# Where a linear-attention block places its last feature-map rows and num/den tiles among the units of the output projection

## The chip, the core and the metric

The kernel runs on one core of a Trainium2 chip. A core has five engines that run side by side, each with its own in-order stream of instructions: TensorE (PE) multiplies matrices, VectorE (DVE), ScalarE (ACT) and GpSimd (POOL) work on elements, SyncE (SP) here only issues DMAs. ACT issues some DMAs too. The metric is the device time of one execution in microseconds; lower is better.

## The reference

`x` is 2048 tokens by 1024 features. It is normalised once, and two blocks read the result:

```python
qkv = (xn @ wqkv)                 # 32 heads of 32
phi = lambda t: where(t > 0, t + 1, exp(t)) + 1e-6
pq, pk = phi(q), phi(k)
kv  = einsum("bhsd,bhse->bhde", pk, v)      # over all tokens
z   = einsum("bhsd->bhd", pk)
num = einsum("bhqd,bhde->bhqe", pq, kv)
den = einsum("bhqd,bhd->bhq", pq, z)[..., None] + 1e-6
s   = (num / den) @ wo                       # heads put side by side again
g   = silu((silu(xn @ w_gate) * (xn @ w_up)) @ w_down)
out = x + s * g
```

Since `kv` and `z` are sums over all tokens, no `num` can be made before the keys and values of the last token are there.

## The kernel before

**Stages.** First the normalisation, K and V for 16 token tiles of 128, and six of the eight Q groups (lines 255 to 596). Then, in lines 598 to 720, the stage that the change is in: the last two Q groups, num/den, and the output projection of the attention. Then the gate, up and down projections (lines 728 to 1064), which take most of the time.

**Q groups.** A `QGroup` (line 205) makes 256 of the 1024 columns of q for 1024 tokens by a seven-product scheme, as phi(q) transposed, in a tile `pqT`. `part_a`, `part_b` and `part_c` issue 8, 12 and 8 matmuls of 128x512; ACT makes exp and relu of the results (lines 186, 187), DVE the sums between them (lines 231, 236, 246). `part_d(i)` closes one of the two rows of 128 columns: `emit_phi` (line 189), two DVE instructions on 128x1024. The two groups of this stage are `qa` and `qb`, the third and fourth column groups of the second half of the tokens.

**num/den tiles.** `emit_ND(b, t)` (line 621) makes one token tile: eight matmuls of 128x132 (line 632) into three PSUM tiles `nd_ps`, all three buffers of the pool `psA`; then on DVE three additions (line 636), a reciprocal (line 639) and three multiplications out of PSUM (line 642) into `o_sb`. The next tile's matmuls need those three buffers back. There are 16 tiles, called tile 0 to 15 below. Tiles 0 to 7 read `pqT` of the first half of the tokens, tiles 8 to 15 that of the second half, `qa` and `qb` included.

**The way to the projection.** `emit_OT` (line 651) takes every finished `o_sb`: ACT issues a write to DRAM (`o_dram`, line 655), SP then issues a transposing DMA back into SBUF (line 656; into `oT` for tiles 0 to 7, into the space of `wq_sb` for 8 to 15). After tile 15 it also puts the first three pairs of gate and up weights into SP's queue (`load_w`, line 658).

**Units.** `emit_S(b, t, cc)` (line 661) is one unit of the output projection: eight matmuls of 128x512 (line 669) for one token tile and one half of the columns, then an ACT cast to `s_sb`; the second unit of a tile also issues the write of `s_sb` on ACT's queue. Units 0 to 31 run in order; unit u reads the transposed tile u//2. Their PSUM comes from `psB`, five buffers, shared with the Q groups.

**Order.** In lines 689 to 720 the order of the instructions on PE, DVE, ACT, POOL and SP is that of the text (`manual_schedule`). `units` and `nds` are the queues of what is still to be issued. Before the loop three tiles are taken; in the loop a tile goes ahead of a unit unless the number of units left is 2 modulo 4, where up to two of the three rows left over stand instead:

```python
rows = deque(((qa, 1), (qb, 0), (qb, 1)))
while units:
    if len(units) % 4 != 2:
        nd_tile()
    else:
        for _ in range(min(2, len(rows))):
            grp, i = rows.popleft()
            grp.part_d(i)
```

So tiles 3 to 15 stand ahead of units 0, 1, 3, 4, 5, 7, 8, 9, 11, 12, 13, 15 and 16; the row (qa, 0) ahead of `qb.part_b`, (qa, 1) and (qb, 0) ahead of unit 2, (qb, 1) ahead of unit 6. `sum_w(0, 0)` and `sum_w(0, 1)` (line 166, DVE sums of the first gate and up weights) stand ahead of unit 28 in both kernels.

Of the kernel before, what the change touches and what calls it, by code (L numbers as in the profile page):

```python
# [21 lines left out]
def kernel(  # L22
# [119 lines left out]
    def x_operands(p):  # L142
        xs, xn_ = XS[p], xnT[p]
        return {"M4": lambda k: xs[:, 0, k, :], "M3": lambda k: xs[:, 1, k, :], "M1": lambda k: xs[:, 2, k, :],
                "N7": lambda k: xs[:, 3, k, :], "N6": lambda k: xs[:, 4, k, :],
                "M5": lambda k: xn_[:, HD + k, TB:2 * TB], "M2": lambda k: xn_[:, k, 0:TB]}
# [19 lines left out]
    def sum_w(m, gu):  # L166
        wsum[(m, gu)] = ws_all[:, m % 2, gu]
        for op in wsum_ops(wraw[(m, gu)], wsum[(m, gu)]):
            op()

    def w_operands(m, gu):
        return block_operands(wraw[(m, gu)], wsum[(m, gu)])

    def load_w(m, after=None, sync=False):
        cols = slice(m * FW, (m + 1) * FW)
        wg_sb = wgu.tile([P, DC, FW], BF16, name="wg_sb", tag="wg_sb")
        d1 = nc.sync.dma_start(out=wg_sb[:], in_=wg_v[:, :, cols])
        wu_sb = wgu.tile([P, DC, FW], BF16, name="wu_sb", tag="wu_sb")
        d2 = nc.sync.dma_start(out=wu_sb[:], in_=wu_v[:, :, cols])
        gate([d1, d2], after, sync=sync)  # L180
        wraw[(m, 0)] = wg_sb
        wraw[(m, 1)] = wu_sb
# [72 lines left out]
    with ExitStack() as p1:  # L255
# [242 lines left out]
        with tc.manual_schedule(engines=FRONT_ORDER):  # L498
# [69 lines left out]
            for i in range(TPB, NT):  # L568
                grp = QGroup(*early.popleft()) if i >= Q0 and early else None
# [28 lines left out]
    with ExitStack() as p2:  # L598
# [9 lines left out]
        def oT_of(b):  # L608
            return (oT_ab[:] if b < 2 else oT_cd)[:, b % 2]

        def emit_KVZ():
            for j in range(NJ):
                g0 = j * GPT
                ng = min(GPT, G - g0)
                nc.vector.tensor_tensor(out=KVZ[:, g0:g0 + ng, 0:P], in0=kvz_ps[j][:, 0:ng, 0:P],
                                        in1=mask[:, None, :].to_broadcast([P, ng, P]), op=ALU.mult)
                nc.vector.tensor_tensor(out=KVZ[:, g0:g0 + ng, P:P + HPG],
                                        in0=kvz_ps[j][:, 0:ng, P:P + 1].to_broadcast([P, ng, HPG]),
                                        in1=sel[:, None, :].to_broadcast([P, ng, HPG]), op=ALU.mult)
# [31 lines left out]
        def emit_OT():  # L651
            while o_ready:
                b, t, o_sb = o_ready.popleft()
                r0 = b * TB + t * P
                nc.scalar.dma_start(out=o_dram[r0:r0 + P, :], in_=o_sb[:])
                nc.sync.dma_start_transpose(out=oT_of(b)[:, :, t * P:(t + 1) * P], in_=o_dram[r0:r0 + P, :])
                if (b, t) == (NB - 1, TPB - 1):
                    for m in range(PREF):
                        load_w(m)
# [19 lines left out]
        units = deque((b, t, cc) for b in range(NB) for t in range(TPB) for cc in range(NCC))  # L679
        nds = deque((b, t) for b in range(NB) for t in range(TPB))  # L680

        def s_unit():
            emit_S(*units.popleft())

        def nd_tile():
            if nds:
                emit_ND(*nds.popleft())

        with tc.manual_schedule(engines=FRONT_ORDER | {ET.SP}):

            qa, qb = (QGroup(NPASS - 1, m) for m in (NM_Q - 2, NM_Q - 1))
            for c in range(NCC):
                nc.sync.dma_start(out=wo_sb[:, :, c * CW:(c + 1) * CW], in_=wo_v[:, :, c * CW:(c + 1) * CW])
            emit_KVZ()
            qa.part_a()
            qa.part_b()
            nd_tile()
            qb.part_a()
            emit_OT()
            qa.part_c()  # L700
            nd_tile()
            qa.part_d(0)
            qb.part_b()
            emit_OT()
            nd_tile()
            qb.part_c()
            emit_OT()
            rows = deque(((qa, 1), (qb, 0), (qb, 1)))
            while units:
                if len(units) % 4 != 2:  # L710
                    nd_tile()
                else:
                    for _ in range(min(2, len(rows))):
                        grp, i = rows.popleft()
                        grp.part_d(i)
                if len(units) == 2 * NCC:
                    sum_w(0, 0)
                    sum_w(0, 1)
                s_unit()
                emit_OT()  # L720
    p12.close()
    ps12.close()

# [207 lines left out]
    with tc.manual_schedule(engines=PE_ORDER):  # L931
        prev = None
        for m, p in order:
# [15 lines left out]
            for gu in range(2):  # L949
                sink = gs if gu == 0 else UpSink(gs, m, p)  # L950
                grp = Group(w_operands(m, gu), x_operands(p), HD, sink)
# [92 lines left out]
    with tc.manual_schedule(engines=PE_ORDER):  # L1044
# [9 lines left out]
        for j in range(NPAIR):  # L1054
            grp = nxt
# [39 lines left out]
```

## Time and profile before

| what | value |
|---|---|
| median of three runs | 758.9 us (758.7 to 759.54) |
| the profiled execution's own time | 758.81 us |
| its span, first to last instruction | 757.0 us |
| PE busy / DVE / ACT / POOL | 746.9 / 482.1 / 276.5 / 50.9 us |
| PE, 179.49 to 191.00 us (end of `qb.part_c` to unit 4) | 10.34 of 11.51 us busy |
| PE, 191.00 to 217.00 us (the other tiles) | 25.84 of 26.00 us busy |
| PE, 217.00 to 244.25 us (units alone) | 27.14 of 27.25 us busy |
| granted TensorE clock | 1.00 in these three windows |
| first matmul of the gate projection | 244.25 us |

A profile is of one execution. The span leaves 1.81 us of that execution's time outside. The profile counts a matmul as busy for longer than its share of the array (378 ns where the next one starts 216 ns later), so two matmuls overlap, and what PE loses is better read from the starts than from the busy share.

### The profile page before, as it was taken

Reading aid. Unit: us, or ns where it says so; the run is one execution under the profiler, and the core shown is the slowest. Engines: PE = TensorE matmul, PEld = TensorE weight load, DVE = VectorE, ACT = ScalarE, POOL = GpSimd, SP = SyncE. Lnnn points to the kernel's source line nnn. Section 1 sums busy time; section 2 is a strip of 40 time slices with the busy share of each in tenths; the row PEclk is TensorE's granted clock in tenths of the full one; section 3 lists DMA queues with packets and bytes.
Section 4 is the critical chain, followed back from the end, with each engine's and each line's share of the span. In section 5 each row is a group of like instructions: output and inputs, shape, how many; then the busy total and the mean of one; then the engine's idle time right before and its main releaser. Section 6 shows DMA issues by size and latency. Waiting matters only on the chain.

```text
span 757.0 us, 9915 instructions
## 1 busy us (share of the span) xinstructions
PE 746.9 (99%) x3724; PEld 351.7 (46%) x3764; DVE 482.1 (64%) x897; ACT 276.5 (37%) x482; POOL 50.9 (7%) x112
## 2 busy tenths in 40 slices
PE   8999999999999999999999999999999999999997
PEld 4544444444544444444444444444444444444454
DVE  6686666349843577776787777776755744445453
ACT  4444556555223434343433334343443111111111
POOL 3311000000000000000000000000000112222220
PEclk9999999999999999999999999999999999999999
DMA  9606100016899334573354634543869854554200
GB/s 318 223 16 184 40 1 0 1 45 186 237 234 287 115 102 146 165 217 110 93 174 147 202 107 131 170 150 112 298 225 352 299 181 181 181 178 171 96 29 29
DMA packets 127663, 115.98 MB, mean 153 GB/s; under 512 B 29440, under 2 KB 108416, under 8 KB 126336
## 3 DMA queue, kind: packets, MB, share of 16 engines
q1 hardware_dynamic: 122720, 106.58, 44.8%
q10 hardware_dynamic: 4896, 8.78, 3.5%
q8 instruction: 29, 0.48, 0.3%
q14 instruction: 18, 0.15, 0.1%
HBM read 70.52 MB, written 38.54 MB: 144 GB/s over the span
## 4 chain that ended last, share of the span: by engine, by line
PE 95%; DVE 3%; issue 1%; DMA 0%; ACT 0%; DVEq 0%; ACTq 0%
PE X L131 29%; PE Y L131 28%; PE kv_ps L428 14%; PE Z L131 10%; PE s_ps L669 6%; PE qY L131 3%; PE qX L131 3%; PE kvz L457 1%; PE nd_ps L632 1%; DVE o_sb L642 1%; PE qZ L131 1%; DVE stats L322 0%; PE tr_ps L397 0%; DMA xp<-in_A_x_dram 0%; DVE pqT L191 0%
## 5 line engine op out<-in xcount | busy, mean ns | idle before, releaser
L131 PEld LDWEIGHTS <-ws_all 128*128 128x128 bf16 x1420 | 137.8, 98 | 162.6 <-issue 0.2
L758 DVE TENSOR_TENSOR q<-n,Y 128x512 f32<-128x512 f32 x63 | 43.4, 688 | 116.8 <-PE Y L131 105.8
L428 PE MATMUL kv_ps<-wkv_sb,xnT 128*128 128x512 bf16 x496 | 114.2, 379 | 1.2 <-DVE xnT L411 0.5
L131 PEld LDWEIGHTS <-xs 128*128 128x128 bf16 x616 | 58.0, 98 | 63.1
L1028 POOL TENSOR_TENSOR o_out<-y,xres 128x512 bf16<-128x512 f32 x29 | 33.5, 1157 | 652.4 <-DVE y L1027 652.4
L428 PEld LDWEIGHTS <-xnT 128*128 128x128 f16 x512 | 49.3, 98 | 57.6 <-DVE xnT L411 0.7
L131 PE MATMUL Y<-xs,ws_all 128*128 128x512 f16 (+3 forms) x308 | 70.3, 360 | 0.0
L131 PE MATMUL X<-xnT,ws_all 128*128 128x512 f16 (+1 forms) x278 | 70.1, 379 | 0.2
L131 PE MATMUL Z<-xs,ws_all 128*128 128x512 f16 x224 | 57.5, 379 | 0.0
L131 PE MATMUL Y<-xnT,ws_all 128*128 128x512 f16 x224 | 57.5, 379 | 0.0
L131 PE MATMUL X<-xs,ws_all 128*128 128x512 f16 x224 | 57.5, 379 | 0.0
L882 ACT ACTIVATE g<-cg 128x512 bf16<-128x512 f32 x56 | 35.4, 633 | 53.9 <-DVE cg L773 53.9
L764 DVE TENSOR_TENSOR u<-Z,q 128x512 f32<-128x512 f32 x63 | 43.3, 688 | 16.0 <-PE Z L131 15.9
L882 ACT ACTIVATE g<-X 128x512 bf16<-128x512 f32 x28 | 16.7, 598 | 99.3 <-PE X L131 99.2
L754 ACT COPY n<-X 128x512 f32<-128x512 f32 x63 | 37.0, 587 | 28.2 <-PE X L131 27.8
L907 DVE TENSOR_TENSOR ho<-g,up 128x1024 bf16<-128x1024 bf16 x56 | 38.3, 686 | 0.5
L131 PEld LDWEIGHTS <-wg_sb 128*128 128x128 bf16 x224 | 21.9, 98 | 26.6 <-issue 0.3
L673 ACT CAST s_sb<-s_ps 128x512 bf16<-128x512 f32 x32 | 18.4, 587 | 43.4 <-PE s_ps L669 29.5
L131 PEld LDWEIGHTS <-wu_sb 128*128 128x128 bf16 x224 | 21.9, 98 | 26.4
L1027 DVE TENSOR_TENSOR y<-y,s_in 128x512 f32<-128x512 f32 x31 | 21.3, 686 | 20.2 <-ACT y L1021 15.9
L1021 ACT ACTIVATE y<-X 128x512 f32<-128x512 f32 x8 | 4.8, 598 | 69.7 <-PE X L131 61.2
L186 ACT ACTIVATE e_t<-kv_ps 128x512 bf16<-128x512 f32 x32 | 19.2, 600 | 29.6 <-PE kv_ps L428 27.2
(140 smaller groups left out, 1046.1 us busy)
## 6 DMA issues: line engine op xcount, KB each, us to landing
h_dram<-ho SPq DMA_DIRECT2D x56, 256.0 KB, 2.5
wg_sb<-in_B_w_gate_dram SPq DMA_DIRECT2D x14, 512.0 KB, 4.0
wu_sb<-in_B_w_up_dram SPq DMA_DIRECT2D x14, 512.0 KB, 4.0
wdr<-in_B_w_down_dram SPq DMA_DIRECT2D x14, 512.0 KB, 4.0
ws_all<-h_dram SPq DMA_DIRECT2D x4, 1792.0 KB, 8.3
wds_dram<-wdsA SPq DMA_DIRECT2D x14, 384.0 KB, 2.6
hp_a<-h_dram SPq DMA_DIRECT2D x3, 1792.0 KB, 9.0
o_dram<-o_sb ACTq DMA_DIRECT2D x16, 256.0 KB, 3.1
```

The lines of the kernel that those rows point to most:

```text
L131: marks["mm"] = nc.tensor.matmul(acc[:, 0:c1 - c0], lhsT=lhs(k), rhs=rhs(k)[:, c0:c1], start=(first and k == 0), stop=(k == n - 1), skip_g ...
L186: nc.scalar.activation(out=e, in_=t, func=ACT.Exp)
L428: mm = nc.tensor.matmul(kv_ps[:], lhsT=xn_tok_ap(i)[:, dc, :], rhs=wkv_sb[:, dc, c * CW:(c + 1) * CW], start=(dc == 0), stop=(dc == DC - 1))
L669: mm = nc.tensor.matmul(s_ps[:], lhsT=oT[:, c, ttok], rhs=wo_sb[:, c, cc * CW:(cc + 1) * CW], start=(c == 0), stop=(c == G - 1))
L673: nc.scalar.copy(out=s_sb[:, cc * CW:(cc + 1) * CW], in_=s_ps[:])
L754: nc.scalar.copy(out=n[:], in_=self.X[:])
L758: nc.vector.tensor_tensor(out=self.q[:], in0=n[:], in1=self.Y[:], op=ALU.add)
L764: nc.vector.tensor_tensor(out=self.u[:], in0=Z[:], in1=self.q[:], op=ALU.add)
L882: nc.scalar.activation(out=self.g[:, i, j * TB:(j + 1) * TB], in_=src, func=ACT.Silu)
L907: nc.vector.tensor_tensor(out=self.ho[:, i], in0=self.g[:, i], in1=self.up[:, i], op=ALU.mult)
L1027: nc.vector.tensor_tensor(out=t[:], in0=t[:], in1=self.s_in[:, i, cs], op=ALU.mult)
L1028: (nc.vector if last and (i, j) != (0, 0) else nc.gpsimd).tensor_tensor(out=self.o_out[:, i, cs], in0=t[:], in1=self.xres[:, i, cs], op=AL ...
```

## The change

Three statements move; no instruction is added or dropped.

```diff
             qa.part_c()
             nd_tile()
-            qa.part_d(0)
             qb.part_b()
...
-            rows = deque(((qa, 1), (qb, 0), (qb, 1)))
+
+            rows = deque((grp, i) for grp in (qa, qb) for i in range(2))
+            nd_at = {1, 2, 4, 6, 8, 10, 11, 12, 14, 15, 16, 18, 19}
+            row_at = {3, 5, 7, 9}
+            assert len(nd_at) == len(nds) and len(row_at) == len(rows)
+            u = 0
             while units:
-                if len(units) % 4 != 2:
+                if u in nd_at:
                     nd_tile()
-                else:
-                    for _ in range(min(2, len(rows))):
-                        grp, i = rows.popleft()
-                        grp.part_d(i)
+                if u in row_at:
+                    grp, i = rows.popleft()
+                    grp.part_d(i)
                 if len(units) == 2 * NCC:
                     sum_w(0, 0)
                     sum_w(0, 1)
                 s_unit()
                 emit_OT()
+                u += 1
```

Tiles 3 to 15 now stand ahead of units 1, 2, 4, 6, 8, 10, 11, 12, 14, 15, 16, 18 and 19. Unit 0 follows `qb.part_c` with nothing between. The four rows stand one each ahead of units 3, 5, 7 and 9. The writes, the transposes and the weight loads that hang on the tiles move with them.

## The prediction

> **What bounds the kernel now.** I read the page first, then the chain of waits over this stage, the waits, PE's timeline, DVE's timeline, and the DMA issues one at a time.
>
> ```profile
> span 757.0 us, 9915 instructions
> PE 746.9 (99%) x3724; PEld 351.7 (46%) x3764; DVE 482.1 (64%) x897; ACT 276.5 (37%) x482; POOL 50.9 (7%) x112
> ```
>
> PE is the bound nearly everywhere; only what PE loses can be won. The waits from 179 to 217 us say where that is: PE waits for the multiplications that empty the num/den buffers.
>
> ```profile
> PEld L632 <- DVE o_sb L642: 3.5, 9, 0.9
> ...
> PE nd_ps L632 <- DVE o_sb L642: 0.7, 2, 0.4
> ```
>
> PE's timeline gives the places (start, length, what):
>
> ```profile
> 179.98 1.09 PE L632 MATMUL nd_ps<-KVZ,pqT 128*128 128x132 bf16 x8 [0.33 <-DVE o_sb L642]
> 180.91 1.89 PE L669 MATMUL s_ps<-wo_sb,oT 128*128 128x512 bf16 x7
> 183.18 1.08 PE L632 MATMUL nd_ps<-KVZ,pqT 128*128 128x132 bf16 x8 [0.39 <-DVE o_sb L642]
> 184.10 3.61 PE L669 MATMUL s_ps<-wo_sb,oT 128*128 128x512 bf16 x16
> 187.55 0.63 PE L632 MATMUL nd_ps<-KVZ,pqT 128*128 128x132 bf16 x8
> 188.02 1.89 PE L669 MATMUL s_ps<-wo_sb,oT 128*128 128x512 bf16 x8
> 189.82 1.08 PE L632 MATMUL nd_ps<-KVZ,pqT 128*128 128x132 bf16 x8
> ```
>
> Tile 5 (187.55) costs PE 0.47 us, start to start; tiles 3, 4 and 6 cost far more. DVE's timeline says why:
>
> ```profile
> 176.90 0.42 DVE L190 TENSOR_SCALAR e_t<-e_t 128x1024 bf16<-128x1024 bf16 x1
> 177.42 0.69 DVE L191 TENSOR_TENSOR pqT<-e_t,pqT 128x1024 bf16<-128x1024 bf16 x1
> 178.03 0.68 DVE L236 TENSOR_TENSOR qu<-qu,qZ 128x512 f32<-128x512 f32 x1
> 178.63 0.31 DVE L636 TENSOR_SCALAR rden<-nd_ps 128x12 f32<-128x12 f32 x3
> 178.98 0.35 DVE L639 RECIPROCAL rden<-rden 128x32 f32<-128x32 f32 x1
> 179.36 1.35 DVE L642 TENSOR_TENSOR o_sb<-nd_ps,rden 128x384 bf16<-128x384 f32 x3
> ```
>
> The row (qa, 0), 176.90 to 178.03, stands ahead of tile 2's work, so tile 2's buffers come free late and tile 3 waits; tile 4 waits for tile 3 in the same way, and tile 6 for tile 5, which the two rows ahead of unit 2 had pushed back.
>
> **What is lost, from PE's starts.** In the chain 16 matmuls of two units take 3.45 us, 0.2157 each, so a unit takes 1.726. `qb.part_c` ends at 179.49 (last start 179.270 plus 0.216). Tile 3: 179.49 to 180.905, 1.42 against 0.47, loses 0.95. Tile 4: 182.63 to 184.10 loses 1.00. Tile 6: 189.75 to 190.75 loses 0.53. Six more tiles (7, 9, 10, 12, 13, 15), each one unit behind the one before it, take 0.60 and lose 0.13 each, 0.77. Sum 3.25. Control: 179.49 to 216.47 is 36.98, less 16 units (27.62) and 13 tiles (6.11) is 3.25. From 245 us on, PE's starts show no stall worth a term.
>
> **The change, part by part.**
> *Row (qa, 0) away from `qb.part_b`, unit 0 ahead of tile 3.* DVE's sum at 178.03 can start at 176.90, tile 2's multiplications end at about 179.7 instead of 180.7, and tile 3's matmuls come at 179.49 + 1.73 = 181.21. Tile 3's 0.95 goes. What stands behind it is unit 0 at 179.49: its tile 0 was issued for transposing at 175.66 and took 3.3, so landed at 178.9. Cover 0.5 us.
> *Tile 4 ahead of unit 2.* It starts at 183.41, DVE is through with tile 3 at about 183.75; the three buffers come free one after the other, as with the tiles that take 0.60. Of its 1.00, 0.13 stays.
> *Tiles 5 to 8 two units apart, a row between.* Two units and a tile are 3.92 us; DVE needs 2.2 for a tile (rows above: 0.31 + 0.35 + 1.35 with gaps) and 1.13 for a row. No wait: tile 6's 0.53 goes. The last row precedes tile 8's matmuls by about half a microsecond, and only the last of the eight reads it.
> *Neighbouring tiles.* 1-2, 10-11, 11-12, 14-15, 15-16, 18-19 are six pairs at 0.13, 0.77 as before; tile 4's 0.13 is one of them. So stalls on `nd_ps` fall from 3.25 to 0.77: a gain of **2.48**.
> *The transposes.* Units 0 to 4 now come earlier, tiles 3 and later do not all. Needs: unit 4 at 187.93 (179.49 + 4 units + tiles 0.47, 0.60, 0.47) wants tile 2; unit 6 at 191.87 wants tile 3. Tile 2's write is issued behind four ACT exp/relu, 183.20 before; DVE reaches their input 0.97 earlier, so 182.23. Tile 3's write stands on ACT behind unit 1's cast and that tile's own s write, 1.24 after the unit's end (185.83 and 187.07 before): 183.41 + 1.24 = 184.65. What a trip takes:
>
> ```profile
> o_dram<-o_sb ACTq DMA_DIRECT2D x1, 256.0 KB, 2.1
> oT<-o_dram SPq DMA_TRANSPOSE x1, 3.2
> ...
> o_dram<-o_sb ACTq DMA_DIRECT2D x1, 256.0 KB, 4.0
> oT<-o_dram SPq DMA_TRANSPOSE x1, 4.5
> ```
>
> The first two are tile 1's, alone in the queues (177.41, 179.51); the others are issues around 190.7 and 191.0, with an s write and an o write under way. Tile 2's write goes out alone: 2.1, so 184.32. Its transpose meets the s write (184.22) and tile 3's write (184.65): between 3.0 and 4.5, four like cases 4.05, 4.07, 4.14, 4.54. I take 4.1: landed 188.4, unit 4 waits **0.5** (bounds 0 and 0.9; with a write of 2.8, as at 172.85, 1.6). Tile 3's trip: 7.1 to 8.7 from issue to landing in the trace, mostly 7.9: 192.55 against 192.4 then: another **0.2**. Unit 8 wants tile 4 (issued about 186.2, landed 194.1) at 196.5; units 10, 12 and 14 have 1.6 us or more in hand, later ones over 3.
>
> The Trainium skill ("Advanced Engine Details and Errata", X-Bar Transpose) calls transposes as fast as plain DMAs on trn2; the trace has 3.2 against 2.1 for the same 256 KB. By that rule both waits go and the sum is 2.48. Another page speaks against the change ("DMA: Bandwidth & Descriptors", Latency and other measured facts): HBM access 0.2 us on average, 2 us at high load. Estimated from it, 1.8 more on each of two transfers, tile 2 would land at 191.1, unit 4 would wait 3.2, and the change would lose 0.7.
>
> *SP and what follows.* Tile 15 now leaves behind unit 19 (its cast, an s write): its write goes out at about 222.85 and the first weight load at 227.45, against 223.24 before, 4.2 late. On POOL nothing is passed. The second pair's up weights landed at 235.2 and DVE summed them until 236.95; now about 241.15. DVE's next work is the first gate sum, 2.29 after the units' end: 244.8. Cover 3.6; the first pair has more (sums done near 237, wanted at 244). Past the cover it would cost one for one. The s writes meet the weights later, over fewer units; five PSUM buffers hid them before. Nothing here costs. Three rows moved behind units cost DVE the same 1.13 each, hidden under matmuls.
>
> **Sum.** 2.48 - 0.7 = 1.78. Against the execution's own 758.81 that is 757.03; the median shown is 0.09 higher, so **757.1**. Own range 756.3 to 758.0.
>
> **Rivals.**
> *No wait at all for the transposes.* For: tile 2's queue is empty ahead of it, and such trips took 5.1 to 5.3. Against: an s write is issued 0.1 us before its transpose. Gain 2.48: **756.4**.
> *Both transfers at the long end.* Tile 2 in 2.8 + 4.5: unit 4 waits 1.6, tile 3 is then in time. Gain 0.88: **758.0**, no difference to be told. For: those lengths are in the trace. Against: both at once for a write that meets no other.
> *A wait takes the stalls' place and outweighs them (slower).* Place: units 4 and 6, on `oT`; PE's order is fixed, so tiles and units behind them wait too. Price: each microsecond over 187.93 or 191.87 is one on the end. Level with before when the two together reach 2.48: tile 2's trip 8.2 or tile 3's 9.7. At tile 3's trip of 12.2 the wait is 5.0 and the time **761.4**. For: ACT issues tile 3's write behind other work. Against: the longest trip is 8.7.
> *The stalls stay*, DVE being 12.04 of 13 us busy from 181 to 194: against it, the same DVE work is spread over three more units, and no two rows stand together any more. Were tiles 3 and 4 to wait as before, 0.53 + 0.13 would be left: 758.2.
>
> **How the numbers follow.** Forecast 0.48, no wait 0.17, long end and stalls that stay together 0.20, slower 0.15. A difference of 0.2% (1.52 us, so below 757.38) is about what can be told from none. Of the forecast some 0.38 lie below that, with 0.17 from the first rival: faster 0.56. Same: the rest of the forecast, most of the third group, a little of the last: 0.28. Slower 0.16. Range 755.9 to 759.8: from the no-wait case with the last 0.77 half gone, to a wait of 3.4.
>
> **What would show it.** Tile 3 at about 181.2 without idle time before it; no wait of PE for `o_sb` over 0.2 us; unit 4 and unit 6 starting right as the transposes of tiles 2 and 3 land, near 188.4 and 192.6; the first gate matmul near 242.5 instead of 244.25, and everything behind it shifted by the same. It would be wrong if a wait stood at units 8 to 14, if DVE's gate sum waited for weights, or if the gate stage changed its length.

## The result and the profile after

| | before | after |
|---|---|---|
| median | 758.7 us (19 runs, 758.58 to 759.54) | 757.39 us (19 runs, 756.84 to 758.93) |
| the profiled execution | 758.81 us, span 757.0 | 756.84 us, span 755.1 |
| end of `qb.part_c` to first gate matmul (below: the stage) | 64.61 us | 62.78 us |
| first gate matmul to last matmul | 507.92 us | 507.79 us |

The ratio is 0.9984, 95% interval [0.9977, 0.9991]: 1.3 us of the median. The profiled execution is 1.97 us under that of before; it is also the shortest of the 19. The stage is taken on PE's starts (179.49 to 244.09 before, 179.46 to 242.24 after; the chain of waits puts the first gate matmul 0.16 later). It holds 1.83 of those 1.97 us.

PE's timeline of the changed kernel, to be read against the seven rows shown of before:

```profile
179.46 1.89 PE L669 MATMUL s_ps<-wo_sb,oT 128*128 128x512 bf16 x7
181.19 0.63 PE L632 MATMUL nd_ps<-KVZ,pqT 128*128 128x132 bf16 x8
181.66 1.89 PE L669 MATMUL s_ps<-wo_sb,oT 128*128 128x512 bf16 x8
183.38 0.77 PE L632 MATMUL nd_ps<-KVZ,pqT 128*128 128x132 bf16 x8
184.34 3.63 PE L669 MATMUL s_ps<-wo_sb,oT 128*128 128x512 bf16 x16 [0.19 <-DMA oT<-o_dram]
187.81 0.63 PE L632 MATMUL nd_ps<-KVZ,pqT 128*128 128x132 bf16 x8
188.78 3.40 PE L669 MATMUL s_ps<-wo_sb,oT 128*128 128x512 bf16 x15 [0.34 <-DMA oT<-o_dram]
192.01 0.63 PE L632 MATMUL nd_ps<-KVZ,pqT 128*128 128x132 bf16 x8
192.48 3.61 PE L669 MATMUL s_ps<-wo_sb,oT 128*128 128x512 bf16 x16
```

No tile waits any more: the bracket with DVE's multiplications is gone from every num/den row, tile 3 starts at 181.19, tile 6 at 192.01 right behind unit 5. (Tiles one unit behind the one before them still take 0.60 instead of 0.47, as at 183.38.) Two brackets of another kind stand at units 2 and 4. Unit 2 could have begun at 183.98 (tile 4 at 183.38 plus 0.60) and began at 184.34 behind a transpose that landed at 184.30; that is 0.36 us. Unit 4 (one of its records is missing, so its row begins with the second matmul) ran until 192.01, so it began at 192.01 - 2 x 1.726 = 188.56 instead of 187.81 + 0.47 = 188.28: 0.28 us. The waits from 179 to 217 us say the same:

```profile
PEld L669 <- DMA oT<-o_dram: 0.7, 2, 0.4
PE s_ps L669 <- DMA oT<-o_dram: 0.5, 2, 0.3
```

These two stand where the two rows "L632 <- DVE o_sb" stood; the 4.2 us of these (weight loads and matmuls counted together) are not there at all.

### The profile page after: what moved, and what is told of

It is laid out like the page before. It is cut to its first block, busy times and chain, and to the rows that moved or that the text cites. A ratio compares the mean times of both kernels' runs of the same rounds, so it can differ in the third digit from the quotient of the medians.

```text
span 755.1 us, 9916 instructions
## 1 busy us (share of the span) xinstructions
PE 745.4 (99%) x3724; PEld 351.9 (47%) x3764; DVE 482.9 (64%) x897; ACT 276.3 (37%) x482; POOL 52.6 (7%) x112
## 4 chain that ended last, share of the span: by engine, by line
PE 95%; DVE 2%; DMA 1%; ACT 1%; issue 1%; DVEq 0%; ACTq 0%
PE X L131 29%; PE Y L131 28%; PE kv_ps L428 14%; PE Z L131 10%; PE s_ps L669 6%; PE qY L131 3%; PE qX L131 3%; PE kvz L457 1%; PE qZ L131 1%; PE nd_ps L632 1%; DVE stats L322 0%; DMA oT<-o_dram 0%; PE tr_ps L397 0%; DMA o_dram<-o_sb 0%; DMA xp<-in_A_x_dram 0%
## 5 line engine op out<-in xcount | busy, mean ns | idle before, releaser
L1032 POOL TENSOR_TENSOR o_out<-y,xres 128x512 bf16<-128x512 f32 x29 | 35.2, 1214 | 648.8 <-DVE y L1031 648.8
```

What stands on the lines that cost most here:

```text
L1032: (nc.vector if last and (i, j) != (0, 0) else nc.gpsimd).tensor_tensor(out=self.o_out[:, i, cs], in0=t[:], in1=self.xres[:, i, cs], op=AL ...
```

## The experiments

Each was run against the kernel before, which ran between its runs on the same chip. "Stage" is from each one's profile; it leaves out the start of the kernel, which alone moved the end of `qb.part_c` between 179.4 and 180.3 us in these profiles.

| kernel | median, us | before then | ratio [95%] | stage, us |
|---|---|---|---|---|
| changed, again | 757.0 | 759.06 | 0.9976 [0.9965, 0.9987] | 63.02 |
| changed, third time | 757.33 | 758.88 | 0.9982 [0.9973, 0.9990] | 62.80 |
| units 2 to 7 on tile 0 | 756.93 | 759.06 | 0.9968 [0.9956, 0.9980] | 62.12 |
| tiles alone | 757.71 | 759.06 | 0.9987 [0.9978, 0.9997] | 63.44 |
| one row alone | 758.28 | 758.87 | 0.9993 [0.9984, 1.0002] | 64.22 |
| tile 2's write early | 758.04 | 759.06 | 0.9986 [0.9977, 0.9994] | 62.98 |
| six matmuls ahead | 757.17 | 758.87 | 0.9980 [0.9971, 0.9989] | 62.78 |
| both | 758.44 | 758.87 | 0.9987 [0.9978, 0.9996] | 64.37 |
| six matmuls ahead, on before | 758.88 | 758.87 | 1.0001 [0.9992, 1.0010] | 64.61 |
| early head | 756.39 | 758.88 | 0.9966 [0.9953, 0.9978] | see below |
| early head, spaced | 756.59 | 758.88 | 0.9971 [0.9959, 0.9984] | see below |
| and weights early | 764.32 | 758.71 | 1.0070 [1.0057, 1.0084] | see below |

### What the stalls were worth: no unit waits for a transpose

```diff
-            ttok = slice(t * P, (t + 1) * P)
+            tr = 0 if b == 0 else t
+            ttok = slice(tr * P, (tr + 1) * P)
```

> Units 2 to 7 of the projection read the transposed tile 0 again instead of tiles 1 to 3, so these rows of the output are another computation; all writes and transposes stay. That takes away what units 2, 4 and 6 wait for. Theory A: 2.48 us under the kernel before, so 756.2 to 756.5, with a spread of under 0.5 us as before, and the first gate matmul at 241.6 to 241.8. Rival B: the time of the changed kernel (757.4) and its spread stay.

Four rows of its PE timeline, where the stage begins 0.6 us later than in the profile after (tile 4, units 2 and 3, tile 5, units 4 and 5):

```profile
184.00 0.77 PE L632 MATMUL nd_ps<-KVZ,pqT 128*128 128x132 bf16 x8
184.60 3.61 PE L670 MATMUL s_ps<-wo_sb,oT 128*128 128x512 bf16 x16
188.05 0.63 PE L632 MATMUL nd_ps<-KVZ,pqT 128*128 128x132 bf16 x8
188.52 3.61 PE L670 MATMUL s_ps<-wo_sb,oT 128*128 128x512 bf16 x16
```

The stage is 62.12, 2.49 us under before: the 2.48 of the sum to a hundredth. The median, 756.93, is above what was expected (2.13 under before on its chip), and not by the stage: in its profile the stage began at 180.08, 0.6 later than in the profile of before, from waits in the first 11 us, one of them for a weight load (0.30 us). The spread, 756.0 to 757.25 in six runs, was wider than expected too. So the part of the claim that rests on the stage is shown, the time of 756.2 to 756.5 was not reached.

### The changed kernel again

> The changed kernel as it is, to see another execution's waits. Theory A (the stalls on the num/den buffers went, 2.48 us, and the transposes gave part back at units 2 and 4, by a different amount in each execution): time 757.0 to 758.0, wider spread than the kernel before; the idle time of PE ahead of units 2 and 4 differs from the first profile's 0.33 and 0.28 us, and the span differs by the same. Rival B (something behind the stage costs the rest, the stage itself is the same in each execution): units 2 and 4 wait as in the first profile within 0.1 us, and the length from the first gate matmul to the end differs.

> The changed kernel once more, on the same chip as the two versions with an early head, as the one to compare them with, and for another execution's waits. Theory A: stage 62.5 to 63.5, idle time ahead of units 2, 4 or 6 of 0.3 to 1.2 us in all, time 757.0 to 757.6.

In the second profile unit 2 did not wait; unit 4 waited 0.55 us (188.09 to 188.64) and unit 6 0.33 (192.57 to 192.90, tile 3 having landed at 192.85). In the third, unit 4 alone waited, 0.63 us (187.85 to 188.48). The rows of units 4 and 6 in the second and PEld's waits there, then unit 4 in the third. A bracket counts from the modelled end of the matmul before, so it is shorter than the wait taken from the starts. Unit 6's bracket names an ACT cast, but PEld, the weight load ahead of the matmuls, waited 0.56 us for the transpose at unit 4 and 0.34 at unit 6, together the 0.9:

```profile
188.64 3.63 PE L669 MATMUL s_ps<-wo_sb,oT 128*128 128x512 bf16 x16 [0.39 <-DMA oT<-o_dram]
192.90 3.63 PE L669 MATMUL s_ps<-wo_sb,oT 128*128 128x512 bf16 x16 [0.17 <-ACT s_sb L673]
...
PEld L669 <- DMA oT<-o_dram: 0.9, 2, 0.6
...
188.48 3.63 PE L669 MATMUL s_ps<-wo_sb,oT 128*128 128x512 bf16 x16 [0.47 <-DMA oT<-o_dram]
```

In the three profiles the waits are 0.64, 0.88 and 0.63 us, and the stage was 62.78, 63.02 and 62.80 us: what it has over the run on tile 0 is these waits and a few hundredths. Theory A holds, with another share for units 2, 4 and 6 in each execution. Rival B has a small part as well: in the second profile the second product of the gate projection stood still, which lengthened what follows the stage by 0.48 us (508.27). Its row in PE's timeline:

```profile
244.01 1.02 PE L131 MATMUL Y<-xs,wg_sb 128*128 128x512 f16 x4 [0.31 <-ACT s_sb L673]
```

Its PSUM buffer was held by one of ACT's last two casts, which waited until 243.3 for an s write; with the weight loads under way that write took 6.1 us, where the first s writes of this profile took 2.3 and 2.4. In the first profile this cost nothing, in that of before 0.13.

### Tiles alone, and one row alone

Tiles in their new places with the rows nearly as before (`tiles_only`, shown against the changed kernel), and the kernel before with one row moved (`row_late`, shown against the kernel before):

```diff
             nd_tile()
+            qa.part_d(0)
             qb.part_b()
...
-            rows = deque((grp, i) for grp in (qa, qb) for i in range(2))
+            rows = deque(((qa, 1), (qb, 0), (qb, 1)))
-            row_at = {3, 5, 7, 9}
+            row_at = {5, 7, 9}
```

> The tiles in their new places, but the row (qa, 0) ahead of qb.part_b as before and the other three rows ahead of units 5, 7 and 9. Theory A: tiles 3, 4 and 6 lose their stalls by their places alone (tile 4 loses about 0.2 instead of 0.13), but tile 2's write goes out 0.97 us later and unit 4 waits for it that much longer: 757.6 to 758.3. If the row (qa, 0) was what held tiles 3 and 4 back, their stalls stay: 758.2 or more, with PE waiting 0.3 us or more for o_sb at tile 3.

```diff
-            qa.part_d(0)
...
-            rows = deque(((qa, 1), (qb, 0), (qb, 1)))
+            rows = deque(((qa, 0), (qa, 1), (qb, 0), (qb, 1)))
```

> The kernel before with one edit alone: the row (qa, 0) leaves its place ahead of qb.part_b and joins the others ahead of unit 2 (two there, two ahead of unit 6). Theory A (by the rows of the kernel before): tile 3's 0.95 us goes, tile 4 still waits for tile 3's multiplications (about 0.95), tile 6 for the two rows (0.4 to 0.5); units 2 and 4 come late enough for their transposes: stage 0.9 to 1.2 us shorter, 757.8 to 758.2. Rival (the places of the tiles did all): tile 3 waits as before, no change.

The tiles alone do most: stage 63.44, 1.17 less than before. Tile 3 does not wait, tile 4 loses 0.22; but unit 4 waits 1.22 us (188.43 to 189.65), since the row holds tile 2's write back to 183.61:

```profile
189.65 3.63 PE L669 MATMUL s_ps<-wo_sb,oT 128*128 128x512 bf16 x16 [1.05 <-DMA oT<-o_dram]
```

That is what moving the row adds: 0.66 of the stage.

The row alone brought 0.39 where 0.9 to 1.2 was expected. Tile 3's stall goes, as expected; a new one comes at tile 8, which needs the row (qb, 1) and finds two rows ahead of it. This row of PE's timeline of `row_late` is the last matmul of tile 8, the waiting one:

```profile
196.53 0.23 PE L632 MATMUL nd_ps<-KVZ,pqT 128*128 128x132 bf16 x1 [0.44 <-DVE pqT L191]
```

So one row each at units 3, 5, 7 and 9 is a part of the change that works: with all four in pairs, the stall only moves.

### Why tile 1 came late: the instruction queue

In the profile of before tile 1's transpose took 3.2 us, in that of after 4.7, though it was issued at the same time (179.51, 179.56) and the next write only at 183.2 and 182.2. The DMA view of 179 to 184 us of both (GB/s moved in 40 slices of 0.125 us, then the instruction queue and the transpose). Before:

```profile
GB/s 66 0 0 0 0 0 0 0 0 0 0 0 0 0 45 129 211 270 182 186 246 160 250 277 91 49 2 131 0 0 0 0 0 0 0 0 0 0 0 0
...
q8 instruction: 1, 0.02, 1.1%
...
oT<-o_dram SPq DMA_TRANSPOSE x1, 3.2
```

After:

```profile
GB/s 99 0 0 0 0 0 0 0 0 0 0 0 0 0 137 109 150 170 143 125 180 109 39 0 0 0 0 2 6 10 8 10 10 8 162 293 289 324 470 360
...
q8 instruction: 1, 0.02, 2.2%
...
oT<-o_dram SPq DMA_TRANSPOSE x1, 4.7
```

The one packet of 16 KB on queue 8, the instruction queue, began at 182.47 in the first, when the transpose's last packet was through (182.28), and at 180.77 in the second, just ahead of its first packet (180.86). There the transpose runs nearly dry for 1.4 us (181.75 to 183.12). Its records hold transpose packets of up to 1.8 us, against 0.018 us for most, and the 16 KB packet itself takes 1.74 instead of 0.88. Two runs move the instruction stream a little (`shift6` on the changed kernel, `shift6_before` on the one before), one issues tile 2's write early (`early_write`), and one does both (`shift6_early`):

```diff
-            warm_up(14)
+            warm_up(13)
+            for _ in range(7):
+                nc.tensor.matmul(w_ps[:, 0:64], lhsT=warm[:, 0:P], rhs=warm[:, 0:64], start=True, stop=True)
```

> The changed kernel with six more matmuls at the very start, in idle time: one warm-up matmul of 512 columns is replaced by seven of 64. Nothing else moves, but PE's instruction stream is six pairs further on everywhere, so the 16 KB fetch of the instruction queue that fell at 180.8 us, in the middle of tile 1's transpose, should fall near 179.5. Theory C (the fetch is what makes tile 1's transpose 3.8 to 4.7 us instead of 3.2): the transpose takes 3.2 to 3.4, unit 2 does not wait, the stage is 0.0 to 0.4 us shorter than in the changed kernel's profiles (62.77 and 63.02), 756.6 to 757.2. Rival D (the write of tile 2 behind it slows the transpose): still 3.8 or more, unit 2 waits.

> Control: the kernel before with the six matmuls alone. Its trips have room, so no change: within 0.3 us of the kernel before, stage 64.5 to 64.7.

```diff
             nd_tile()
+            emit_OT()
             qb.part_c()
-            emit_OT()
```

> The write of tile 2 to DRAM is issued ahead of the four exp/relu of qb.part_c on ACT instead of behind them, so at 179.75 instead of 182.22 us. Theory A: tile 2 is transposed by about 186, unit 4 no longer waits (0.3 us in the first profile, more in the median); unit 2's wait for tile 1 stays or grows a little: 756.6 to 757.1. Rival B: no change, 757.4. A third way: the earlier write slows tile 1's transpose, unit 2 waits longer, 757.4 or more.

> The same six matmuls together with tile 2's write ahead of the exp/relu of qb.part_c. Theory C: tile 1's transpose is not blocked, takes 3.2 to 3.6 although the write overlaps it, tile 2 lands by 186.5; no unit waits, stage 62.1 to 62.3 as with the units that read tile 0: 756.2 to 756.7. Rival D: tile 1's transpose takes 4.5 or more, unit 2 waits 0.5 us or more, no gain over the changed kernel.

The DMA view of the same window in `shift6` and then in `early_write` has

```profile
oT<-o_dram SPq DMA_TRANSPOSE x1, 3.4
...
o_dram<-o_sb ACTq DMA_DIRECT2D x1, 256.0 KB, 4.6
oT<-o_dram SPq DMA_TRANSPOSE x1, 5.3
```

With the six matmuls the 16 KB packet fell at 180.49 (not near 179.5, as expected), ahead of most of the transpose, which took 3.4, and unit 2 did not wait: theory C's prediction for this run. But unit 4 then waited 0.66 us, for tile 2 that landed at 188.71, and the time did not move: what one trip won, the next one lost here. The control, the same matmuls on the kernel before, changed nothing: stage 64.61.

The early write gained nothing: its median is 1.0 us above the changed kernel's on the same chip (757.0), though in its one profile the stage, 62.98, is no longer than there. Tile 1's transpose took 5.3 us, tile 2's write 4.6 instead of 2.1 to 2.8, and unit 2 waited 0.86 us (184.75 to 185.61): the third way of the expectation. With both edits tile 1's transpose took 4.8, the write 4.4, and unit 2 waited 0.44; in that profile, which is of the longest of its 11 runs, tile 3's transpose took 5.9 and unit 6 waited 1.64. So theory C fell for this run, where rival D is right in the main: a write issued 0.2 us behind a transpose goes with a longer trip of both. How much of the transpose is the write's doing is not separated: the 16 KB packet, begun 0.55 us after the transpose's issue, still ran for the first 0.6 us of its packets, about as long as in the second profile of the changed kernel, where the transpose took 3.8.

Over the nine profiles of this stage without an early write or an early head, tile 1's transpose took 3.2 to 3.4 when the 16 KB packet began 0.65 us after its issue or more than 2.5 us after, and 3.8 to 4.7 when it began 1.0 to 2.2 us after. In the five with the long transposes tile 2's write is hardly a rival cause: its first packet moved between 0.3 us ahead of the end of the transpose's last packet and 0.2 us behind it. That a trip is longer with either thing in its way is shown by these runs, most of them one profile each; how it comes about inside the DMA engines is not.

### A version with more room, and how far it goes

The way out is to start the trips earlier, not to make them shorter. The first four tiles go forward among the Q groups:

```diff
             qa.part_a()
+            nd_tile()
             qa.part_b()
+            emit_OT()
             nd_tile()
             qb.part_a()
             emit_OT()
             qa.part_c()
             nd_tile()
             qb.part_b()
             emit_OT()
             nd_tile()
+            emit_OT()
             qb.part_c()
-            emit_OT()
...
-            nd_at = {1, 2, 4, 6, 8, 10, 11, 12, 14, 15, 16, 18, 19}
+            nd_at = {2, 4, 6, 8, 10, 11, 12, 14, 15, 16, 18, 19}
```

> The changed kernel with the first four num/den tiles further forward: tile 0 ahead of qa.part_b, tile 1 ahead of qb.part_a, tile 2 ahead of qb.part_b, tile 3 ahead of qb.part_c, each write issued as soon as its tile is done; tiles 4 to 15 stay where the change puts them. Theory A: every trip to DRAM and back starts 2 to 4 us earlier, so units 2, 4 and 6 don't wait for a transpose whatever its length, and the pair 3-4 is gone (0.13): stage 61.9 to 62.1, time 756.1 to 756.6, spread under 1 us. If the sums of the Q groups on DVE or the exp/relu on ACT are pushed back by the tiles, PE waits at qa.part_c or qb.part_c instead, 757 or more.

> The same head, and tiles 4 to 15 two units apart as far as it goes (ahead of units 1, 3, 5, 7, 9, 11, 13, 15, 17, 18, 20, 21; rows ahead of 2, 4, 6, 8). Theory A: of the six pairs at 0.13 two are left, stage 61.5 to 61.7, 755.7 to 756.3, as long as tiles 7 to 11 are transposed in time (they leave 7 units ahead of their use and need about 10.6 us of 12). Rival: one of these waits for its transpose, or the first weights, now 2 units later than in the changed kernel, are late for the gate stage: 757 or more.

Since a tile leaves the stage here, the comparison is from the last K/V matmul to the first gate matmul: 79.09 us before, 77.25 to 77.50 in the three profiles of the changed kernel, 76.47 with the early head, 76.07 spaced. The early head has the lowest median of all: 756.39 us, 0.9966 of before, its five runs within 0.62 us, as expected; no row of PE's timeline from 164 to 222 us names a DMA. By the same measure the run on tile 0 has 76.60; less the 0.13 of the pair that is gone here, that is 76.47, so no unit lost time to a transpose. Its interval meets that of the changed kernel, and the two were not timed against each other, only against before on one chip (757.33 there).

Spaced, the stage won the further 0.40 us, and gave it back at once: tile 15 and the weight loads behind it leave two units later, DVE sums the second pair of weights until 244.5 and only then gets to the gate's first sum, which empties the PSUM buffer that PE's fifth gate product, the second into a `Y`, is waiting for. That is the rival of the expectation. PE's row, 0.66 us late:

```profile
245.17 1.02 PE L131 MATMUL Y<-xnT,ws_all 128*128 128x512 f16 x4 [0.49 <-DVE q L764]
```

The last run puts two pairs of weights ahead:

```diff
-                if (b, t) == (NB - 1, TPB - 1):
-                    for m in range(PREF):
+                if b == NB - 1 and t in (0, TPB - 1):
+                    for m in (range(2) if t == 0 else range(2, PREF)):
                         load_w(m)
```

> The version with the early head and spaced tiles, with one more edit: the loads of the first two pairs of weights go into SP's queue behind tile 12's transpose instead of behind tile 15's, some 10 us earlier; the third pair stays behind tile 15. In the spaced version PE waited 0.66 us at the second gate product because DVE summed late weights ahead of the gate's first sum. Theory A: that wait goes, units 24 to 31 still get their tiles in time: last K/V matmul to first gate matmul 76.0 to 76.2, gate stage back to 507.8, time 755.7 to 756.2. Rival: the weights slow the transposes of tiles 13 to 15 or the s writes so much that units 26 to 30 or ACT's casts wait: 756.5 or more.

764.32 us, 0.7% slower than before: the rival, far beyond its size, and mostly by a way that it did not name, the order in SP's queue. Two rows of SP's timeline, one of PE's, and three windows (from left: length, PE, PEld, DVE, ACT and POOL busy, granted clock, DMA share, GB/s):

```profile
225.37 3.19 SPq L179 DMA_DIRECT2D wu_sb<-in_B_w_up_dram  x1
228.61 8.62 SPq L656 DMA_TRANSPOSE wq_sb<-o_dram  x3
...
237.14 12.43 PE L669 MATMUL s_ps<-wo_sb,wq_sb 128*128 128x512 bf16 x48 [6.19 <-DMA wq_sb<-o_dram]
```

```profile
225.00:231.00 6.00, 5.95 (x28) 2.49 (x26) 1.70 (x4) 1.19 (x3) 0.00 (x0) 1.00 1.10 346
231.00:237.00 6.00, 0.00 (x0) 0.00 (x0) 4.26 (x10) 1.05 (x2) 0.00 (x0) 0.76 1.22 210
237.00:243.00 6.00, 5.86 (x19) 2.33 (x20) 0.83 (x3) 0.89 (x2) 0.00 (x0) 0.67 0.92 229
```

SP is in order and the loads' issues took until 228.6, so the transposes of tiles 13 to 15 could not be issued before, though tile 13's write had landed at 221.1. Its transpose landed at 237.1, 8.5 us after its issue. Against the spaced version it was issued 7.4 us later (221.2 there) and took 1.3 longer (7.2 there): standing behind the loads' issues cost far more than the slower trip. PE did nothing for 6.2 us, and the granted clock fell to 0.76 and then 0.67: the last six units took 12.26 us, where 48 matmuls at 0.2157 are 10.35. The wait at the gate did go, as theory A had it (507.79 from the first gate matmul to the last), but the stretch before the gate is 84.32 us instead of 76.07.

## Why the prediction was right, point by point

**The stalls on the num/den buffers, 2.48 us.** Right: tile 3 at 181.19 (said: 181.2), no wait for `o_sb`, six pairs at 0.60 left, and 2.49 with the transposes out of the way. Theory and size are shown by the run on tile 0.

**What the transposes take back, 0.7 us.** Right in sum, 0.64, 0.88 and 0.63 in three profiles, and partly wrong in place, so the agreement of the first profile is in part luck. Unit 4 was named and waits in all three, 0.28 to 0.63 against 0.5 said. The 0.2 at unit 6 came in one of them (0.33); in the first, tile 3 landed at 190.81, not 192.55. And unit 2 has no term in the prediction: with tile 1's landing of before (182.72) it would have had 1.3 us in hand, but in the first profile that tile landed at 184.30. Trips outside the given bounds came elsewhere too: tile 3's was 6.2 us in the first profile (bounds 7.1 to 8.7), tile 7's 9.3, which left unit 14 1.0 us instead of 1.6 or more, and tile 13's 10.1. The weak step is treating trips measured once as fixed lengths or bounds.

**The sum.** 757.03 was said for the profiled execution, which took 756.84; 757.1 for the median, which is 757.39, with 757.0 and 757.33 in the other two series. The gate's first matmul came at 242.40 by the chain of waits (said: 242.5). Against before, the medians of the three series gained 1.31, 2.06 and 1.55 us where 1.78 was said, so the remaining 0.3 us are within what series differ by. The three medians lie around 757.38, the mark below which the prediction would call the change faster, with 0.56. The runs spread over 2.1 us in 19, against 1.0 before. It may be that PE now waits for DMAs, whose lengths differ from run to run, where it waited for DVE. That the early head, where no unit waits, is back at 0.62 us over five runs agrees with this; the run on tile 0, where none waits either, spread over 1.25 in six, which speaks against it. The cause of the spread stays open.

**SP and what follows: "Nothing here costs".** The loads left at 228.38 (said: 227.45) and DVE's sums ended at 242.1 (said: 241.15), the gate's first sum came at 244.44. The cover was 2.3 us, not 3.6, and it held; the spaced version shows that it is real and what is past it costs. What the prediction missed is the wait for ACT's last casts: 0 to 0.48 us at the gate's second product, in some executions.

**The rivals.** No wait at all (756.4) is what the run on tile 0 did to the stage and the early head to the time. Both transfers at the long end (758.0) is close to single runs of 758.2 to 758.9, but none of these was profiled, so what they waited for is not shown. The slower case, a wait on the transposes that outweighs the stalls, did not come with this change; a wait of that kind, at later units, is what the last run shows, where SP's order made tile 13's trip 19 us (218.1 to 237.1). Stalls that stay: no.

**The two rules weighed.** Transposes as fast as plain DMAs (the Trainium skill, "Advanced Engine Details and Errata", X-Bar Transpose (TRN2)) did not hold for single transfers of 256 KB: 3.0 to 3.4 us undisturbed against 2.1 to 2.8 for the write, which goes the other way, and 2.7 for the quickest plain load of that size in the same trace. The 1.8 us more per transfer that the prediction estimated from the other page's HBM latency at high load ("DMA: Bandwidth & Descriptors", Latency and other measured facts), which would have made the change lose, is too much for this stage: in the three profiles tile 2's write took 2.1 to 2.8 us and its transpose 3.5 to 4.1, against 2.1 and 3.0 before.

## What to carry to other kernels

When a stall on a buffer is removed, work out what the next unit needs and when that was issued: here a gain of 2.5 us met DMA trips with no time in hand and kept 1.3 to 2. A DMA trip that the critical engine waits for is a distribution, not a number (tile 3's took 6.2, 7.8 and 8.0 us in three profiles of one kernel); give it room by issuing the work that feeds it earlier, and put nothing long ahead of it in an in-order DMA queue. And spread both kinds of work: the rows that helped one at a time brought a new stall in pairs.

## What the runs showed of the hardware that was not expected

- A 16 KB packet of the instruction queue that falls into a small DMA holds it up: tile 1's transpose took 3.8 to 4.7 us with it, 3.2 to 3.4 without. Adding six short matmuls at the start moved that packet forward, against the end of `qb.part_c`, by 0.4 to 0.5 us in the changed kernel and by 0.2 in the one before.
- A 256 KB write issued 0.2 us behind a 256 KB transpose took 4.4 to 4.6 us instead of 2.1 to 2.8, and the transpose 4.8 to 5.3 (two runs, with the 16 KB packet near by in both).
- In one run, after 6.2 us in which PE had nothing to do, the granted clock was 0.67 on average over the next 6 us.
